# Holding transfers back during attention bursts, loading the third token tile ahead of the first query weights, and narrower last pieces, with a new table of shifts, in a fused attention and SwiGLU layer

## The chip, the cores and the metric

The kernel runs on one core of a Trainium2 chip. The metric is the device time in microseconds (us) of one execution. Times below are medians of several executions; a profile is one execution, and its span is about 1.7 us shorter than that execution's time. The engines are called PE (matrix products), DVE, ACT, POOL and SP, which here only issues transfers.

## The reference, cut to what matters

```python
# S = 2048 tokens, D = 1024, H = 32 heads of 32, N = 4 segments of L = 512, F = 3584, all bf16
for s in range(4):                       # per segment: local softmax and a memory of the past
    p = softmax(qs @ ks.T * scale + causal_mask);  a_dot = p @ vs
    a_mem = (phi(qs) @ M) / (phi(qs) @ z + 1e-6)
    o = g * a_mem + (1 - g) * a_dot
    M = M + phi(ks).T @ vs;  z = z + sum(phi(ks))
h  = x + o @ wo                          # q, k, v come from layernorm(x)
out = h + (silu(ln(h) @ w1) * (ln(h) @ w3)) @ w2
```

## The kernel before

The kernel writes operations into a graph. A small planner with its own cost model then decides the order on every engine, and a table SHIFT, with entries for 470 of 472 units of work, nudges that order. The table is the result of a search. What the chip does is fixed by the orders and the semaphores that the planner emits.

Attention of one segment and half of the heads (eight times in all) runs in ten *score tenancies* (products q k into four PSUM banks, then one exponential on ACT), with dense products of other stages between them, and then one *burst*: the denominators, four numerator columns j = 0 to 3, and in the first three segments the memory product of 64 small products.

```python
    def scores(self, s, g0, i, parts, at):           # one tenancy, i = 0..9
        ...
        o = self.mark = self.g.op("pe", 30.0 + 512 / 2.4, emit, reads=reads, cls=0, group=gr, gate="att")
        ...                                          # exponential on ACT, causal select on POOL

    def finish(self, s, half, at):                   # the burst
        ...
        column(Both(gd, gm) if gm else gd, range(4), lambda i, kc, j: self.ones32[:, j, :], ...)
        for j in range(4):
            gn.append(self.queue(j))
            column(gn[j], [j], lambda i, kc, j: v[:, kc, g0 + i, j, 0:32], j, ...)
        if gm:
            self.memory(s, half, gm)                 # 64 products of 33 columns, one operation
        ...

    def first_half(self):                            # the head
        ...
        loads = [(self.xs[t][:, :], self.x2d[t * 128:(t + 1) * 128, :]) for t in range(4)]
        loads.insert(2, (wq[:, :, 0:256], sq[:, :, 0:256]))
        loads.insert(5, (wk[:, :, 0:256], sk[:, :, 0:256]))
        ...
    # ffn_down, the tail:
        cols = [(0, 512), (512, 256), (768, 256)] if t == 15 else [(0, 512), (512, 512)]
```

The softmax here doesn't subtract the row's maximum and nothing guards it: scores larger than these inputs give would overflow.

Of the kernel before, what the change touches and what calls it, by code (L numbers as in the profile page):

```python
# [21 lines left out]
    0: (113, 0), 1: (-194, 1), 2: (-667, 0), 3: (-97, 0), 4: (-693, -1), 5: (-458, -1),  # L22
    6: (-38, 1), 7: (-273, 0), 8: (-32, 0), 9: (1616, 0), 10: (25, 1), 11: (-286, 1),
    12: (172, -1), 13: (-388, 0), 14: (-1163, 0), 15: (1, -1), 16: (-18, 0), 17: (-393, 0),
    18: (-432, 0), 19: (-332, -1), 20: (-726, 0), 21: (-980, 0), 22: (-590, 0), 23: (-337, 0),
    24: (386, 0), 25: (-423, 1), 26: (-992, 0), 27: (170, 1), 28: (-314, 0), 29: (108, -1),
    30: (-213, 0), 31: (-82, 0), 32: (72, 0), 33: (-46, 0), 34: (-61, 0), 35: (-15, 0),
    36: (66, 1), 37: (-122, 0), 38: (73, 0), 39: (75, 0), 40: (240, 1), 41: (790, 0),
    42: (436, -1), 43: (346, 1), 44: (-203, 0), 45: (-52, 1), 46: (280, 0), 47: (-138, 0),
    48: (-1000, 1), 49: (319, 0), 50: (244, 0), 51: (-194, 0), 52: (-341, 0), 53: (114, 1),  # L30
    54: (236, 0), 55: (443, 0), 56: (472, 0), 57: (-181, 0), 58: (202, 0), 59: (0, 1),
    60: (329, 0), 61: (176, 0), 62: (577, 0), 63: (232, 0), 64: (343, -1), 65: (62, -1),
    66: (-1, 0), 67: (-27, 0), 68: (380, -1), 69: (151, -1), 70: (672, 0), 71: (455, 0),
    72: (333, 0), 73: (389, -1), 74: (-231, 0), 75: (-215, 0), 76: (-1180, 1), 77: (-591, 0),
    78: (60, 0), 79: (105, 1), 80: (-645, 0), 81: (822, 0), 82: (720, 0), 83: (-36, 0),
    84: (290, 1), 85: (278, 0), 86: (781, -1), 87: (738, -1), 88: (264, 0), 89: (-38, 0),
    90: (255, 0), 91: (-292, 0), 92: (489, -1), 93: (276, 0), 94: (340, 0), 95: (-320, 0),
    96: (1003, 1), 97: (-984, 1), 98: (300, -1), 99: (545, 0), 100: (105, 1), 101: (-414, -1),
    102: (1239, 1), 103: (310, -1), 104: (-250, 0), 105: (18, -1), 106: (149, -1),
    107: (-967, 0), 108: (-407, -1), 109: (132, 0), 110: (198, 0), 111: (-185, 0),  # L40
    112: (-466, 0), 113: (484, -1), 114: (-58, 1), 115: (-243, -1), 116: (2, 0), 117: (-382, 1),
    118: (246, 0), 119: (-90, -1), 120: (796, 0), 121: (-239, 1), 122: (350, -1), 123: (22, -1),
    124: (-65, 0), 125: (-125, 0), 126: (75, -1), 127: (-802, 0), 128: (-162, -1),
    129: (-459, 0), 130: (609, 1), 131: (439, 0), 132: (287, 0), 133: (725, 0), 134: (-729, 1),
    135: (-763, 1), 136: (-378, 1), 137: (213, 0), 138: (552, 0), 139: (-94, 0), 140: (666, 0),
    141: (-279, -1), 142: (-1607, 0), 143: (103, 0), 144: (1000, 0), 145: (-281, 1),
    146: (-460, 0), 147: (-775, 0), 148: (-161, 0), 149: (-645, 0), 150: (-119, -1),
    151: (-271, -1), 152: (-125, 1), 153: (-757, 0), 154: (-45, 0), 155: (-1064, 1),
    156: (499, -1), 157: (272, -1), 158: (-539, -1), 159: (-398, 0), 160: (-178, 0),
    161: (-32, 0), 162: (-858, -1), 163: (136, 0), 164: (102, 0), 165: (541, 0), 166: (287, 0),  # L50
    167: (526, 1), 168: (-156, 0), 169: (143, 0), 170: (-57, 1), 171: (232, 0), 172: (-293, 0),
    173: (-111, 0), 174: (-244, 0), 175: (-566, 1), 176: (231, -1), 177: (-352, 0),
    178: (-672, 0), 179: (476, 0), 180: (318, -1), 181: (-30, 0), 182: (-1529, -1),
    183: (442, 0), 184: (314, -1), 185: (-580, 0), 186: (683, -1), 187: (261, -1),
    188: (-351, -1), 189: (-262, 0), 190: (-907, 0), 191: (122, 1), 192: (-381, 0),
    193: (-110, 1), 194: (704, 1), 195: (-226, -1), 196: (996, -1), 197: (-511, 1),
    198: (198, -1), 199: (-599, 1), 200: (-399, 1), 201: (519, 0), 202: (-310, -1),
    203: (10, -1), 204: (-305, 0), 205: (-354, 0), 206: (-422, 1), 207: (-148, 0),
    208: (-508, 0), 209: (-551, 0), 210: (377, 1), 211: (-139, 0), 212: (699, 0), 213: (378, 0),
    214: (236, 1), 215: (424, -1), 216: (-195, -1), 217: (-501, -1), 218: (-302, 1),  # L60
    219: (309, 0), 220: (-919, 0), 221: (321, -1), 222: (24, 1), 223: (-98, 0), 224: (619, 1),
    225: (593, 1), 226: (-320, -1), 227: (-779, -1), 228: (351, 0), 229: (327, 0),
    230: (524, 0), 231: (-389, -1), 232: (-574, 1), 233: (-315, 1), 234: (-277, -1),
    235: (469, 0), 236: (-369, 0), 237: (-511, -1), 238: (180, 0), 239: (-88, 0),
    240: (-241, -1), 241: (-5, 0), 242: (602, 1), 243: (304, 0), 244: (-787, 0), 245: (254, -1),
    246: (449, 0), 247: (1135, -1), 248: (-467, 1), 249: (-501, -1), 250: (130, 1),
    251: (-372, 1), 252: (-158, 0), 253: (1119, 0), 254: (-407, 0), 255: (30, 1), 256: (331, 1),
    257: (-413, 1), 258: (-309, 0), 259: (-293, 0), 260: (93, 1), 261: (200, 1), 262: (852, 0),
    263: (156, 0), 264: (168, 1), 265: (-419, 0), 266: (-101, -1), 267: (995, -1),
    268: (-504, 0), 269: (114, -1), 270: (-156, -1), 271: (230, 0), 272: (-118, 1),  # L70
    273: (-324, 0), 274: (313, 0), 275: (484, -1), 276: (408, -1), 277: (416, 0), 278: (127, 0),
    279: (41, 0), 280: (-85, 0), 281: (-440, 1), 282: (192, -1), 283: (-416, 0), 284: (490, -1),
    285: (-173, 0), 286: (73, -1), 287: (113, 0), 288: (162, 0), 289: (-231, 1), 290: (-91, -1),
    291: (-253, -1), 292: (-197, 0), 293: (-507, -1), 294: (98, 0), 295: (136, 0),
    296: (-846, -1), 297: (-281, -1), 298: (756, -1), 299: (605, 0), 300: (-49, -1),
    301: (266, 0), 302: (222, 0), 303: (163, 0), 304: (15, -1), 305: (7, -1), 306: (171, 1),
    307: (-102, 1), 308: (-164, 0), 309: (573, 0), 310: (36, 1), 311: (-391, -1), 312: (122, 0),
    313: (-258, 0), 314: (-377, -1), 315: (234, 0), 316: (-44, -1), 317: (1293, 1),
    318: (458, 0), 319: (-156, -1), 320: (284, 0), 321: (687, -1), 322: (-244, -1),
    323: (296, 0), 324: (-287, 0), 325: (503, -1), 326: (-600, 0), 327: (447, 0), 328: (409, 0),  # L80
    329: (-186, -1), 330: (17, -1), 331: (-46, 0), 332: (-745, -1), 333: (1259, 0),
    334: (1124, 0), 335: (-208, 0), 336: (-187, 0), 337: (-49, 1), 338: (-90, 0),
    339: (-801, 0), 340: (-433, 0), 341: (19, -1), 342: (229, 0), 343: (-749, 0), 344: (109, 0),
    345: (-144, 0), 346: (795, 0), 347: (79, 0), 348: (-554, 0), 349: (83, 0), 350: (-48, 0),
    351: (-26, -1), 352: (-38, -1), 353: (-200, 0), 354: (-529, 0), 355: (596, 1),
    356: (-272, 1), 357: (259, 0), 358: (330, -1), 359: (258, -1), 360: (345, -1),
    361: (444, 0), 362: (129, 0), 363: (915, 0), 364: (36, 1), 365: (280, 1), 366: (-192, 0),
    367: (208, 1), 368: (829, -1), 369: (19, -1), 370: (-310, -1), 371: (-643, 1),
    372: (-300, -1), 373: (109, 0), 374: (-186, -1), 375: (166, 1), 376: (-1088, 0),
    377: (-657, -1), 378: (-150, 0), 379: (36, 1), 380: (-532, -1), 381: (-323, -1),  # L90
    382: (554, 0), 383: (-401, 1), 384: (-833, 0), 385: (-135, -1), 386: (53, 0), 387: (16, 0),
    388: (548, 0), 389: (-612, 0), 390: (-525, 1), 391: (-475, 0), 392: (-658, 0),
    393: (339, 0), 394: (-515, -1), 395: (-70, -1), 396: (-258, -1), 397: (-860, -1),
    398: (47, 1), 399: (-616, 0), 400: (24, 0), 401: (56, 1), 402: (-245, -1), 403: (4, 1),
    404: (-199, 1), 405: (61, 1), 406: (-1407, -1), 407: (987, 0), 408: (544, 0), 409: (-76, 1),
    410: (194, 0), 411: (-100, -1), 412: (525, 0), 413: (-559, 0), 414: (1023, -1),
    415: (699, 1), 416: (498, 0), 417: (-583, 0), 418: (-521, 0), 419: (-287, 0), 420: (858, 0),
    421: (-596, 0), 422: (-482, 1), 423: (-82, 0), 424: (-41, 0), 425: (-14, 0), 426: (8, 0),
# [11 lines left out]
class Op:  # L110
# [6 lines left out]
    def __init__(self, engs, cost, emit, cls, seq):  # L117
# [16 lines left out]
        self.port = False  # L134
        self.patience = 0.0
        self.offered = 0.0
        self.unit = 0


class Group:  # L140
# [23 lines left out]
class Graph:  # L164
# [128 lines left out]
    def dma(self, out, in_, cls=5, deps=(), eng="sp"):  # L293
        n = 1
# [1084 lines left out]
```

## Time and profile before

| | before |
|---|---|
| time, median of the first 3 runs | 896.3 us |
| span in the profile | 895.0 us |
| PE busy | 880.6 us |
| 512-column products begin (head) | 18.07 us |
| last product ends, span ends (tail) | 892.42, 895.0 us |

The prediction below reads this profile line by line. In a list of groups a line has the engine, the line of the program, output<-inputs, and times; a wait line has who waited <- for what: total us, times, longest us; a chain line has start, duration, and what the end of the program hung on then. In a busy table each engine has its busy time in the stretch, and PE's granted clock, the DMA share and GB/s follow at the end. The timeline of the kernel before has the last addition:

```profile
892.44 0.42 DVE L1289 TENSOR_TENSOR ob<-hr,ps 128x256 bf16<-128x256 bf16 x1 [0.89 <-PE ps L708]
```

### The profile page before, as it was taken

Reading aid. Unit: us, or ns where it says so; the run is one execution under the profiler, and the core shown is the slowest. Engines: PE = TensorE matmul, PEld = TensorE weight load, DVE = VectorE, ACT = ScalarE, POOL = GpSimd, SP = SyncE. Lnnn points to the kernel's source line nnn. Section 1 sums busy time; section 2 is a strip of 40 time slices with the busy share of each in tenths; the row PEclk is TensorE's granted clock in tenths of the full one; section 3 lists DMA queues with packets and bytes.
Section 4 is the critical chain, followed back from the end, with each engine's and each line's share of the span. In section 5 each row is a group of like instructions: output and inputs, shape, how many; then the busy total and the mean of one; then the engine's idle time right before and its main releaser. Section 6 shows DMA issues by size and latency. Waiting matters only on the chain.

```text
span 895.0 us, 13604 instructions
## 1 busy us (share of the span) xinstructions
PE 880.6 (98%) x5833; PEld 403.4 (45%) x5921; DVE 417.6 (47%) x631; ACT 287.9 (32%) x306; POOL 173.8 (19%) x226
## 2 busy tenths in 40 slices
PE   8999999999999999999999999999999999999998
PEld 5343444444444444444444444444444444444445
DVE  5784848585848485754555311211334333331111
ACT  6767766656565646111111100000111111110000
POOL 2553445353534343100200000000000000000000
PEclk9999999999999999999999999999999999999999
DMA  7899755634541221753475211113223221301110
GB/s 235 227 212 271 187 142 147 187 92 130 165 99 57 72 70 58 225 153 92 120 224 140 85 36 36 30 46 90 64 60 94 71 71 48 95 24 41 40 37 30
DMA packets 146540, 96.32 MB, mean 108 GB/s; under 512 B 45488, under 2 KB 133680, under 8 KB 146480
## 3 DMA queue, kind: packets, MB, share of 16 engines
q1 hardware_dynamic: 146480, 95.45, 38.8%
q8 instruction: 47, 0.77, 0.4%
q14 instruction: 13, 0.11, 0.0%
HBM read 76.55 MB, written 8.39 MB: 95 GB/s over the span
## 4 chain that ended last, share of the span: by engine, by line
PE 97%; issue 1%; DVE 1%; DMA 1%; ACT 0%; SPq 0%; ACTq 0%; DVEq 0%
PE ps L708 89%; PE ps L1107 4%; PE ps L1057 3%; DMA xs<-in_A_x_dram 1%; PE ps L985 0%; PE ps L1184 0%; ACT et L1069 0%; PE ps L1100 0%; DVE t L1260 0%; DVE hm L1265 0%; PE ps L720 0%; SPq L299 0%; DVE R L1163 0%; ACT sg L1257 0%; DVE Nsb L1171 0%
## 5 line engine op out<-in xcount | busy, mean ns | idle before, releaser
L708 PE MATMUL ps<-hnT,w1b 128*128 128x512 bf16 x876 | 218.4, 379 | 1.4 <-issue 0.3
L708 PE MATMUL ps<-hnT,w3b 128*128 128x512 bf16 x873 | 217.4, 379 | 1.5 <-issue 0.5
L1257 ACT ACTIVATE sg<-ps 128x512 bf16<-128x512 f32 x112 | 66.9, 597 | 403.1 <-PE ps L708 403.1
L708 PE MATMUL ps<-w2b,hm 128*128 128x512 bf16 (+1 forms) x907 | 195.3, 372 | 0.9
L1069 ACT ACTIVATE et<-ps 128x2048 bf16<-128x2048 f32 x80 | 150.0, 1875 | 39.3 <-PE ps L1057 38.9
L1260 DVE SCALAR_TENSOR_TENSOR t<-sg,ps 128x512 bf16<-128x512 bf16 x112 | 76.8, 685 | 169.4 <-ACT sg L1257 169.2
L708 PEld LDWEIGHTS ps<-w2b,hm 128*128 128x128 bf16 x924 | 90.4, 98 | 103.2
L708 PEld LDWEIGHTS ps<-hnT,w1b 128*128 128x128 bf16 x896 | 86.5, 98 | 105.5 <-issue 8.2
L708 PEld LDWEIGHTS ps<-hnT,w3b 128*128 128x128 bf16 x896 | 86.5, 98 | 105.4 <-issue 2.9
L1078 POOL TENSOR_SCALAR_AFFINE_SELECT et<-et 128x512 bf16<-128x512 bf16 x96 | 84.0, 881 | 126.2 <-ACT et L1069 126.0
L1265 DVE SCALAR_TENSOR_TENSOR hm<-t,ps 128x512 bf16<-128x512 bf16 x112 | 76.7, 686 | 50.5 <-PE ps L708 47.9
L1289 DVE TENSOR_TENSOR ob<-hr,ps 128x512 bf16<-128x512 bf16 (+1 forms) x33 | 22.1, 671 | 143.0 <-PE ps L708 143.0
L708 PE MATMUL ps<-wo,oT 128*128 128x512 bf16 x249 | 60.7, 380 | 0.6 <-issue 0.3
L708 PE MATMUL ps<-xnT,wp 128*128 128x512 bf16 (+1 forms) x345 | 59.7, 320 | 1.4 <-issue 0.6
L708 PE MATMUL ps<-hnT,wp 128*128 128x512 bf16 x250 | 59.0, 380 | 0.7 <-issue 0.6
L708 PEld LDWEIGHTS ps<-xnT,wp 128*128 128x128 bf16 x352 | 27.7, 98 | 26.9 <-issue 3.6
L708 PEld LDWEIGHTS ps<-wo,oT 128*128 128x128 bf16 x256 | 23.9, 98 | 29.8 <-issue 2.9
L708 PEld LDWEIGHTS ps<-hnT,wp 128*128 128x128 bf16 x256 | 23.6, 98 | 29.8 <-issue 3.8
L1200 POOL TENSOR_TENSOR oT<-Nsb,R 128x512 bf16<-128x512 f32 x23 | 35.8, 1569 | 4.1 <-DVE R L1197 4.1
L1163 DVE STREAM_TRANSPOSE R<-Rc 128x1024 f32<-128x1024 f32 x28 | 33.6, 1222 | 0.1
L1229 DVE TENSOR_TENSOR h<-h,ps 128x512 bf16<-128x512 bf16 x32 | 21.7, 680 | 25.1 <-PE ps L708 24.9
L1057 PE MATMUL ps<-qT,kT 32*128 32x128 bf16 (+3 forms) x512 | 31.7, 301 | 0.0
(82 smaller groups left out, 520.9 us busy)
## 6 DMA issues: line engine op xcount, KB each, us to landing
w1b<-in_B_w_dram SPq DMA_DIRECT2D x28, 512.0 KB, 3.9
w3b<-in_B_w_dram SPq DMA_DIRECT2D x28, 512.0 KB, 3.8
wp<-in_A_wv_dram SPq DMA_DIRECT2D x8, 1024.0 KB, 5.5
wp<-in_A_wq_dram SPq DMA_DIRECT2D x7, 1024.0 KB, 5.9
wp<-in_A_wk_dram SPq DMA_DIRECT2D x7, 1024.0 KB, 5.7
w2b<-in_B_w_dram SPq DMA_DIRECT2D x7, 1024.0 KB, 8.0
xs<-in_A_x_dram SPq DMA_DIRECT2D x16, 256.0 KB, 5.6
h<-in_A_x_dram SPq DMA_DIRECT2D x16, 256.0 KB, 3.7
```

Of the source, the lines that this page charges most:

```text
L708: return [e.matmul(p[0](gr), p[1], p[2], start=p[3], stop=p[4]) for p in part]
L1057: ins.append(e.matmul(self.bank(gr, j, 512 - 128 * kc, off), k[r, g0 + g, 128 * kc:128 * kc + 128], q[r, g0 + g, 128 * kc:512], start=True ...
L1069: return [e.activation(et[:, :, :], src, AF.Exp, scale=self.scale)]
L1078: self.pool_op(lambda e, v=v, pat=pat: e.affine_select(v, v, pattern=pat, compare_op=ALU.is_ge, fill=0.0, base=0, channel_multiplier=-1), ...
L1107: ins.append(e.matmul(self.ps[32 * i:32 * i + 32, b * 512 + 128 * kc:(b + 1) * 512], lhsT(i, kc, j), at[i, kc][:, j, :], start=kc == 0 and ...
L1163: return self.dve_op(lambda e: e.transpose(out, src), dve_ns(1024), [Rc[:, t, 2 * n:2 * n + 2, :]], [dst], 2)
L1200: self.either(lambda e, out=out, Ns=Ns, R1=R1: e.tensor_tensor(out, Ns, R1, op=ALU.add), 512, 2, [Ns, R1], [out], 2)
L1229: self.g.op("dve", dve_ns(512), lambda e, gr, hs=hs: [e.tensor_tensor(hs, hs, self.bank(gr), op=ALU.add)], reads=[hs], writes=[hs], cls=1, ...
L1257: self.g.op("act", act_ns(512), lambda e, gr, sg=sg: [e.activation(sg, self.bank(gr), AF.Tanh, scale=0.5)], writes=[sg], cls=0, group=gg)
L1260: e.scalar_tensor_tensor(t1, sg, 1.0, self.bank(gr), op0=ALU.add, op1=ALU.mult)], reads=[sg], writes=[t1], cls=0,
L1265: e.scalar_tensor_tensor(dst, t1, 0.5, self.bank(gr), op0=ALU.mult, op1=ALU.mult)], reads=[t1], writes=[dst], cls=0,
L1289: self.g.op("dve", dve_ns(n), lambda e, gr, hs=hs, ob=ob, n=n: [e.tensor_tensor(ob, hs, self.bank(gr, 0, n), op=ALU.add)], reads=[hs], wri ...
```

## The change

Its intent has three parts. (1) In the plan, no transfer is issued from score tenancy 9 to the numerator product of j = 3, and transfers offered meanwhile get a dependence on that product. (2) Tile 2 of x is loaded before the first query weights, and the planner is given measured scales for the first loads. (3) The last 256 columns of the last tile become two pieces of 128. A new table SHIFT was searched for the changed planner.

```diff
 SHIFT = {
-    0: (113, 0), 1: (-194, 1), 2: (-667, 0), 3: (-97, 0), ...      (nearly every entry differs; cut)
+    0: (60, 1), 1: (-213, 0), 2: (8, 0), 3: (-400, 0), ...
 }
@@ schedule()
                 for e in ENGINES:
-                    if not free[e]:
+                    if not free[e] or e == "sp" and hush:
                         continue
...
                     started.add(o)
+                    hush = o.hush or hush
...
+            if not events and hush:
+                hush = None
+                continue
...
                 n_done += 1
+                if x is hush:
+                    hush = None
+                    for _, _, o in avail["sp"]:
+                        o.deps.setdefault(x, True)
@@ first_half()
+        x = [(self.xs[t][:, :], self.x2d[t * 128:(t + 1) * 128, :]) for t in range(4)]
+        loads = [x[0] + (1.04,), x[1] + (0.7,), x[2] + (1.2,),
+                 (wq[:, :, 0:256], sq[:, :, 0:256], 1.54), x[3] + (0.65,), ...]
@@ scores()
+        if i == 9:
+            self.final = o
@@ finish()
+        self.final.hush = self.mark
@@ ffn_down()
-            cols = [(0, 512), (512, 256), (768, 256)] if t == 15 else [(0, 512), (512, 512)]
+            cols = [(0, 512), (512, 256), (768, 128), (896, 128)] if t == 15 else [(0, 512), (512, 512)]
```

## The prediction

> **What bounds the kernel now.** I read the page first, then the busy time by stretch, the engine waits of PE, the chain of waits, and the timelines of the head, of one burst and of the tail.
>
> From the page:
>
> ```profile
> span 895.0 us, 13604 instructions
> PE 880.6 (98%) x5833; PEld 403.4 (45%) x5921; DVE 417.6 (47%) x631; ACT 287.9 (32%) x306; POOL 173.8 (19%) x226
> PE   8999999999999999999999999999999999999998
> PEclk9999999999999999999999999999999999999999
> DMA  7899755634541221753475211113223221301110
> ```
>
> PE is busy 98% at full clock; only the first and last slices are below 9. At most 895.0 - 880.6 = 14.4 us is idle. A change of transfers and order, with the same products, can win no more unless products themselves get shorter.
>
> The busy time by stretch says where the 14.4 us lie (the first two columns are the stretch and its length, the third is PE's busy time):
>
> ```profile
> 0.00:22.40 22.40, 18.40 (x195) 12.29 (x197) 12.04 (x34) 13.63 (x26) 5.06 (x22) 1.00 0.77 235
> 200.00:300.00 100.00, 97.61 (x921) 42.95 (x930) 66.55 (x94) 63.13 (x56) 46.02 (x52) 1.00 0.41 112
> 500.00:600.00 100.00, 99.53 (x456) 45.39 (x464) 17.33 (x26) 4.18 (x7) 0.00 (x0) 1.00 0.15 43
> 800.00:895.00 95.00, 91.93 (x447) 44.42 (x454) 12.93 (x20) 0.60 (x1) 0.00 (x0) 1.00 0.12 37
> ```
>
> Idle: 4.0 us in the head, 3.07 in the last stretch, and 0.47 per 100 us in the pure feed-forward part (500 to 600). The 0.47 isn't a wait: the chain shows runs of 49 products of 10.74 us, each 10.79 after the one before, so one record in 50 is missing. In 200 to 300 it is 2.39, the largest of the middle. The engine waits of PE name what is left:
>
> ```profile
> PE ps L708 <- issue: 3.0, 19, 0.2
> PE ps L720 <- DVE xs L862: 2.1, 2, 1.2
> PE ps L708 <- DVE oT L773: 1.2, 1, 1.2
> PE ps L985 <- issue: 1.1, 1, 1.1
> PE ps L708 <- DMA wp<-in_A_wq_dram: 0.4, 1, 0.4
> ```
>
> The 19 waits of 0.16 us follow a change between tiled and full-array products and stay. What the change can touch is one gap of 1.1 us at L985 (the memory product), the head's 2.1 + 0.4, and the tail.
>
> The gap, in the chain of waits between 262 and 276 us:
>
> ```profile
> 266.68 2.72 PE ps L1107 x80
> 269.39 0.34 PE ps L985 x42
> 269.73 1.07 issue
> 270.81 0.32 PE ps L985 x22
> ```
>
> The 64 memory products are one operation without a semaphore inside, yet PE stops after 42. Nothing of the program can hold it there: what is missing is the next instruction. In 264 to 271 us the DMA view has one fetch of instructions, an x load that takes 4.6 us to land (median of its kind on the page 3.7) and a transposing transfer that takes 7.4 (median 3.9). The transfers were issued inside the burst.
>
> **The Trainium skill.** (1) "Runtime: NRT & Kernel Launch", Instruction fetch mechanics: instructions stream in 16 KiB blocks of 256, fetched over a DMA queue of the engine's own; crossing a block is "mostly hidden". The trace has such fetches, and here one probably wasn't hidden: the slice 50 to 60 us with its burst takes 216 products and 217 weight loads, an ordinary 10 us 61. (2) "DMA: Bandwidth & Descriptors", Queues, rings and completion order: each DMA engine takes turns between queues, a packet at a time; so a fetch shares with data. The late landings agree with sharing, and don't prove it. (3) "TensorEngine Tiling (Array Packing)", Key Properties: a change of tiling mode drains the engine. Agrees: four dense products take 0.86 us, and a score tenancy starts 0.96 us after four of them began (60.77 to 61.73), so some 0.1 us a change. (4) "DMA: Bandwidth & Descriptors", Specifications: under 512 B a transfer does read-modify-write. The last pieces' rows fall from 512 to 256 B; nothing of this size is in the trace to compare.
>
> **The change, part by part.**
>
> *Silence in the burst.* In the planned order no transfer is issued from score tenancy 9 of a burst to its last numerator product; those offered meanwhile get a dependence on that product, so the silence is real on the chip. No instruction goes. It removes whatever slows fetches in eight bursts. In this trace just one stalled: 1.07 us at most. The others ran 64 memory products in about 0.52 us without a gap, though transfers were in flight at 49.4 to 50.7 (two weights, one x) and 171 to 176 (two weights). I count 0.8 of the 1.07, since the fetch itself remains: **-0.85 us**.
>
> *Head.* Loads go x0, x1, x2, wq, x3, wk instead of x0, x1, wq, x2, x3, wk. The timeline of DVE shows why:
>
> ```profile
> 6.87 0.42 DVE L732 COPY xnT<-ps 128x512 bf16<-128x512 bf16 x1 [0.24 <-PE ps L720]
> 8.34 1.29 DVE L831 BATCH_NORM_STATS2 lnst<-xs 128x6 f32<-128x512 bf16 x2 [1.05 <-DMA xs<-in_A_x_dram]
> 9.55 0.72 DVE L862 TENSOR_SCALAR xs<-xs,lnst,rstd 128x512 bf16<-128x512 bf16 x2
> ```
>
> Tile 1's scale is ready at 7.19 + 0.57 = 7.76 (POOL), but in DVE's order tile 2's statistics stand before its application, and tile 2 lands only at 8.32; so it is applied at 9.55 and PE transposes it at 10.00, after 1.23 us idle. wq lands at 7.70, x2 0.62 later. With the order turned, x2 lands before 6 (x0 at 3.49, x1 at 4.14, so some 0.65 apart, to at most about 1.2) and wq near 7.70 + 0.65 = 8.35. DVE no longer waits: tile 2's statistics fit from 6.6, tile 1 is applied near 8.4, its transposes run near 8.8. PE pays the later wq: idle from 7.30 to about 8.35 instead of 7.70, +0.65; it wins the 1.23 and the 0.20 before 10.92. Net -0.8 at most. But tile 3 still lands at about 9.06 and its chain through ACT sets its transposes at 14.45. After them PE did 52 products in 2.90 us; 32 of them (1.8 us) need tile 3, so only 20 x 0.056 = 1.1 us can come forward. The cap doesn't bind, but a new short wait between tiles is likely. I take **-0.55 us**.
>
> *Tail.* Tile 15's last 256 columns become two pieces of 128. Last addition: 0.69 us at 512, 0.42 at 256; in a straight line 0.29 at 128, -0.13. Transfer: 1.7 us for 128 KB, 1.6 for 64 KB; 32 KB would be 1.55, but may lose it to 256 B rows: 0. PE: 28 products of 256 columns (about 109 ns: half of 213 plus 2.6) become 56 of 128 at 55.8 (1.34 us for 24 in the head), +0.07; there are as many more weight loads, which in the head kept up. Net **-0.05 us**.
>
> *Shifts of all units.* Nearly every entry differs. With PE full between 20 and 887 us, an order can only alter the number of mode changes (80 score tenancies and eight bursts stay) and create waits. I give it **+0.1**; the held transfers below cost +0.2.
>
> Sum: -0.85 - 0.55 - 0.05 + 0.3 = -1.15. A change of this sort is usually kept because it helped, and short issue gaps may go with it; I choose -1.5: 896.3 - 1.5 = **894.8 us**.
>
> **The rivals.** (a) *The silence moves the wait.* Up to three transfers per burst start 5 to 9 us later, together. From 22 to 100 us the DMA share is 1.00 at 240 GB/s, so there a pause isn't free. A weight tile of 1 MB takes 5.5 to 5.9 us to land; with three buffers and 32 products of 216 ns (6.9 us, stretched by attention) on each there are some two tiles of slack, over 13 us. So it should be hidden; if not, one late tile costs 2 to 5 us: 896 to 900. (b) *Transfers were innocent*: the gap is a chance of where a block of instructions ends, so it stays or moves to another burst; then the gain is only head and tail, 895.5 to 896. (c) *The head doesn't gain*: the later wq eats it, +0.65 against 1.43; 895.2 to 895.7. (d) *PE products get faster without transfers*, as if they contended for memory: 49 (with the missing one, 50) in 10.79 us is 216 ns at a DMA share of 0.15 and 1.0 alike (four in 0.86 at 60 us), which speaks against it.
>
> **Range and chances.** Best case: 1.07 + 1.1 + 0.2 + 0.6 of small gaps = 3.0, hence 893.3. Worst likely: one new wait, 896.8. Range **893.3 to 896.8**. Two per cent is 17.9 us, more than all idle time: faster 0.005. Slower by as much would need several starved weights: 0.01. Within: 0.985.
>
> **What would show it.** Right: PE busy within 1 us of 880.6; no issue gap over 0.3 us in the eight bursts; no DMA issue on SP between the tenth score tenancy and the last numerator; PE's transposes of tile 1 before 9.2 us, the wait for wq near 1 us, and the 512-column work starting near 17.4 instead of 18.07; last addition about 0.29. Wrong: PE waits for wp, hnT or wo over 0.5 us after a burst (rival a), a 1 us issue gap anywhere (b), or a head that ends at 18 (c). A busy PE changed by over 3 us would break the ledger itself.

## The result

The changed kernel took 895.03 us (median of 4 runs, 894.24 to 895.94) against 896.49 us (4 runs, 896.26 to 898.08): 1.46 us less. A ratio is the mean time of one kernel's runs over that of the other's of the same rounds, so it isn't quite the ratio of the medians: 0.998, with an interval of 0.9963 to 0.9998. The profiled run of the changed kernel was its fastest (894.24 us), so its span of 892.5 us flatters it by almost 1 us.

The page of the changed kernel, then its busy table (stretch, length, PE, weight loads, DVE, ACT, POOL, clock, DMA share, GB/s):

```profile
span 892.5 us, 13660 instructions
PE 881.4 (99%) x5862; PEld 404.4 (45%) x5949; DVE 426.3 (48%) x645; ACT 282.2 (32%) x296; POOL 171.6 (19%) x223
```

```profile
0.00:22.40 22.40, 20.55 (x206) 13.25 (x208) 13.44 (x34) 14.12 (x26) 5.73 (x23) 1.00 0.79 237
200.00:300.00 100.00, 98.78 (x932) 43.33 (x941) 66.67 (x98) 62.61 (x53) 47.46 (x55) 1.00 0.39 108
```

PE's busy time is as before within 0.8 us: the change took away idle time, not products. In 200 to 300 us PE gained 98.78 - 97.61 = 1.17 us. Its engine waits, with the line L989 of the memory product gone from the list:

```profile
PE ps L711 <- issue: 3.3, 21, 0.2
PE ps L711 <- DVE oT L776: 1.2, 1, 1.2
PE ps L711 <- ACT xnT L734: 0.4, 1, 0.4
```

The timeline shows the memory product of burst 6 in one piece of 0.69 us (64 products; before, 42, then a gap, then 22), and in the head and the tail DVE's lines that answer to those shown before:

```profile
262.95 0.69 PE L989 MATMUL ps<-v,pkn 128*32 128x33 bf16 x64
...
6.36 1.28 DVE L834 BATCH_NORM_STATS2 lnst<-xs 128x6 f32<-128x512 bf16 x2
8.45 0.73 DVE L865 TENSOR_SCALAR xs<-xs,lnst,rstd 128x512 bf16<-128x512 bf16 x2 [0.57 <-POOL rstd L861]
...
890.22 0.29 DVE L1296 TENSOR_TENSOR ob<-hr,ps 128x128 bf16<-128x128 bf16 x1 [0.83 <-PE ps L711]
```

The 2.5 us between the two spans, cut at two marks that both traces have (the start of the 512-column products and the end of the last product):

| stretch | before | after | difference |
|---|---|---|---|
| start to the first 512-column product | 18.07 | 16.99 | -1.08 |
| from there to the end of the last product | 874.35 | 873.21 | -1.14 |
| from there to the end | 2.58 | 2.30 | -0.28 |

So the total was as predicted, and the differences lie in the stretches that it named. Whether for its reasons is what the experiments ask.

### The profile page after: what moved, and what is told of

Same layout as the page of the kernel before. It is cut to its first block, busy times and chain, and to the rows that moved or that the text cites. A ratio compares the mean times of both kernels' runs of the same rounds, so it can differ in the third digit from the quotient of the medians.

```text
span 892.5 us, 13660 instructions
## 1 busy us (share of the span) xinstructions
PE 881.4 (99%) x5862; PEld 404.4 (45%) x5949; DVE 426.3 (48%) x645; ACT 282.2 (32%) x296; POOL 171.6 (19%) x223
## 4 chain that ended last, share of the span: by engine, by line
PE 97%; issue 1%; DVE 1%; ACT 0%; DMA 0%; POOL 0%; SPq 0%; DVEq 0%; ACTq 0%
PE ps L711 90%; PE ps L1113 4%; PE ps L1061 3%; DMA xs<-in_A_x_dram 0%; PE ps L989 0%; PE ps L1191 0%; PE ps L723 0%; PE ps L1106 0%; DVE t L1267 0%; ACT oT L823 0%; ACT sg L1264 0%; ACT oT L820 0%; DVE T L1139 0%; DVE hm L1272 0%; DVE Nsb L1159 0%
## 5 line engine op out<-in xcount | busy, mean ns | idle before, releaser
L711 PE MATMUL ps<-w2b,hm 128*128 128x512 bf16 (+2 forms) x935 | 195.4, 366 | 0.9
L1296 DVE TENSOR_TENSOR ob<-hr,ps 128x512 bf16<-128x512 bf16 (+2 forms) x34 | 22.3, 655 | 142.8 <-PE ps L711 142.8
L1207 POOL TENSOR_TENSOR oT<-Nsb,R 128x512 bf16<-128x512 f32 x21 | 31.4, 1515 | 11.4 <-PE ps L711 6.3
L711 PE MATMUL ps<-wp,xnT 128*128 128x512 bf16 x124 | 31.1, 380 | 0.4 <-issue 0.2
```

Source lines behind the costliest of these rows:

```text
L711: return [e.matmul(p[0](gr), p[1], p[2], start=p[3], stop=p[4]) for p in part]
L1207: self.either(lambda e, out=out, Ns=Ns, R1=R1: e.tensor_tensor(out, Ns, R1, op=ALU.add), 512, 2, [Ns, R1], [out], 2)
L1296: self.g.op("dve", dve_ns(n), lambda e, gr, hs=hs, ob=ob, n=n: [e.tensor_tensor(ob, hs, self.bank(gr, 0, n), op=ALU.add)], reads=[hs], wri ...
```

## The experiments

**How fetches of instructions were read.** The trace also has the transfers of the instruction queue of PE, one per 256 instructions. To set them against the program I numbered PE's instructions in the program's order (a product is two, a weight load and a matmul; a separate wait is one) and matched them to the weight loads in the trace, none of which is missing. The gap of the kernel before then stands right before instruction 5313, and 5313 = 20 x 256 + 193. In the kernel before each of the 47 fetches falls within 4.5 us of the moment when PE passes a number 193 + 256 k, one fetch for each such number; taken in this order, each brings the block that begins at the next one. This gives, per burst, when PE entered a block, when the fetch of the next one ran, and when PE went on with that next block. The rows here are worked out in this way from the traces of all runs of this section:

```
run              burst  enters block  fetch ran         went on   fetch later by   gap
before             6     266.13      268.55 - 269.52    270.80        2.42        1.07
after              6     260.73      260.57 - 261.53    263.47       -0.16        none
before_hold        6     277.65      277.81 - 278.84    281.07        0.16        none
before_hold1       6     266.10      268.34 - 269.49    270.80        2.25        1.10
before_holdT       6     266.76      268.22 - 269.30    270.60        1.47        0.2
before_shift72     1      56.09       59.04 -  60.25     61.46        2.95        1.91
before_shift72     2      96.49      100.16 - 101.25    102.83        3.67        3.09
after_noise        4     170.93      174.45 - 175.41    176.80        3.52        2.15
after_noise        6     263.86      266.43 - 267.49    269.00        2.56        2.21
after_nohush       5     214.14      220.63 - 221.63    223.03        6.49        1.20
```

Wherever there is a gap, it stands at a number of the form 193 + 256 k, and PE goes on 1.2 to 1.6 us after the record of the fetch ends. A late fetch alone makes no gap: in the changed kernel three fetches at bursts 1, 2 and 4 come 3.8, 3.5 and 4.0 us late, but their blocks last 9.2, 7.8 and 15.3 us, and PE doesn't stop. The block of burst 6 lasts 2.75 us there, and its fetch is prompt.

**1. Move the ends of the blocks (before_shift72).** Nothing but the place of the block ends changes.

```diff
             ins = o.emit(engine, o.group)
+            if e == "pe" and o.pos == 0:
+                for _ in range(144):              # emitted as 72 instructions
+                    engine.wait_ge(sems["dve"], 1)
```

> The kernel before with 72 more instructions on PE that only look at a semaphore already reached, right after the 12 warm-up products, in time that PE spends waiting for x; every order and transfer is as before, only the ends of the 256-instruction blocks move by 72. Theory (a block of instructions that runs out in a burst faster than the next one is fetched): the gap at product 43 of the memory product of burst 6 is gone; block ends now stand 24 products after the memory product of burst 2 and 35 after that of burst 1, so a gap of 0.5 to 2 us comes at one or both of those places, and the time is within 1 us of before, either way. Rival (something in burst 6 itself, as a hazard or the DVE): the gap stays in burst 6 after 42 memory products.

Measured: 905.69 us (ratio 1.0097). The chain of waits in bursts 1 and 2:

```profile
57.92 1.10 PE ps L1110 x32
59.02 0.54 PE ps L711 x2
59.56 1.91 issue
...
98.81 0.93 PE ps L1110 x23
99.73 3.09 issue
```

The gap in burst 6 is gone, and two larger ones stand where they were foretold: 34 products after the memory product of burst 1 and 23 after that of burst 2 (35 and 24 were named). PE lacks instructions there; nothing in burst 6 itself is at fault. The expected time was wrong by 8 us: the two gaps cost 5.0 us, the 72 instructions held the head up by 2.7 us (a third gap of issue; the clock fell there too, to 0.50 in 10 to 12 us), and after the 3.09 us gap the clock was halved. The busy table (PE alone, then clock, DMA share, GB/s) shows it:

```profile
102.00:104.00 2.00, 1.17 (x11) 0.50 0.65 148
104.00:106.00 2.00, 2.00 (x6) 0.50 0.82 216
```

**2. Put transfers into the bursts of the changed kernel (after_noise).** Two useless copies of 1 MB, issued after score tenancy 9 of bursts 4 and 6.

```diff
+    for b in (3, 5):
+        first = self.bursts[b]                     # score tenancy 9
+        for k in range(2):
+            ...                                    # dma scratch <- x, 512 rows, deps = {first: True}
```

> The changed kernel with two useless 1 MB copies from x to a scratch in memory, issued when the last score tenancy of burst 4 and of burst 6 is done (the result stays right, no order changes). Theory: they delay the fetch in those bursts. In burst 6 the fetch now starts 0.2 us before PE enters the block and ends 1.9 us before PE needs the next; it comes 1 to 3 us later, and a gap of 0.5 to 2.5 us shows where the block ends, just after the memory product of burst 6, perhaps another in burst 4; span 0.5 to 3 us longer than the changed kernel. Rival (transfers innocent): no gap over 0.3 us in these bursts, span within 0.3 us unless PE waits for a named transfer.

Measured: 899.23 us (ratio 1.0025). The chain of waits in burst 4, then 6:

```profile
174.35 0.30 PE ps L1009 x37
174.65 2.15 issue
...
266.26 0.52 PE ps L1009 x64
266.78 2.21 issue
```

Both fetches come 3.5 and 2.6 us late, and PE has two gaps of 4.4 us together. Against the span of 893.8 us in experiment 5, which ran on the same chip with the same orders on the other engines, its 898.0 us are 4.2 us longer, more than the 0.5 to 3 expected because both bursts stalled. Transfers in a burst, here plain copies, delay the fetch, and this makes the gap: shown.

**3. The silence alone (before_hold).** All orders of the kernel before stay; only the waits are added.

```diff
+    for first, last in self.bursts:                # tenancy 9, numerator j = 3
+        for o in sp:
+            if first.start <= o.start < last.start and all(u.start >= last.start for u in o.users):
+                o.start = last.start + 1e-6 * k    # keeps SP's order
+                o.deps[last] = True
```

> The kernel before with every engine's order untouched; only the transfers that its plan starts between score tenancy 9 of a burst and that burst's numerator product j=3 get a wait on that product (the change's silence and nothing else). Theory (the 1.07 us gap in the memory product of burst 6 is PE short of instructions, because the fetch of the next block queued behind transfers issued in the burst): the fetch that started 2.4 us after PE entered block 5057 starts within 0.5 us of it, the gap at L985 is gone, span 0.7 to 1.2 us shorter than the kernel before. Rival (transfers innocent, the gap belongs to the place where the block ends): the gap stays at about 1.1 us and the time is the same within 0.3 us. Second rival (the silence moves the wait): gap gone, but PE waits over 0.5 us for a weight or hnT.

Measured: 914.67 us, ratio 1.02 (1.0187 to 1.0214). The fetch is prompt and the gap gone (third row of the table), but the engine waits of PE now begin so:

```profile
PE ps L723 <- DMA hnT<-hn: 4.7, 1, 4.7
PE ps L723 <- DMA wp<-in_A_wv_dram: 4.7, 1, 4.7
PE ps L723 <- DMA h<-in_A_x_dram: 3.2, 2, 2.8
PE ps L735 <- DVE xs L877: 1.5, 2, 1.0
PE ps L723 <- DMA wp<-in_A_wq_dram: 1.5, 1, 1.5
```

For late transfers PE waits 4.7 + 4.7 + 3.2 + 1.5 = 14.1 us, all but 0.3 of it right after a burst, and after the two long waits the clock falls (0.62 and 0.53 in the two stretches of 4 us after 188 us), which lengthens the products there. First theory and second rival are both true: the silence heals the gap, and by itself moves more wait than it heals.

**4. Which transfer? (before_hold1, before_holdT).** In burst 6 of the kernel before three transfers are in the way: w3b (issued 262.70), the transposing transfer hnT (263.12) and an x load (266.40). Of the held ones, one run holds the last alone, the other the transposing one alone.

```diff
-    for first, last in self.bursts: ...
+    first, last = self.bursts[5]
+    held = [o for o in sp if first.start <= o.start < last.start]
+    held[-1].start = last.start + 1e-6             # before_holdT: held[-2]
+    held[-1].deps[last] = True
```

> The kernel before, all orders untouched; of all transfers just one, the 256 KB x load of burst 6 (issued at 266.4 us, landing 4.6 us later), waits for that burst's numerator product j=3. Theory that this load delayed the fetch: the fetch of the next block starts under 1 us after PE enters block 5057 instead of 2.4, the gap of 1.07 us at L985 is below 0.3 us, and no weight is late, so 0.7 to 1.2 us shorter than the kernel before. Rival (the transposing transfer issued at 263.1 us delayed it): the fetch still comes over 2 us late and the gap stays near 1 us; time the same.

Measured: 896.57 us, ratio 0.9995 (0.9983 to 1.0007), the same. I named the x load as the cause, and it isn't: in the chain of waits the gap stays.

```profile
269.36 0.34 PE ps L997 x42
269.70 1.10 issue
```

> The kernel before with one transfer of burst 6 held until numerator product j=3: the transposing transfer of normalised rows (hnT) that was issued at 263.1 us and took 7.4 us to land; the x load of that burst goes ahead of it. All other orders are untouched. Theory (the transposing transfer delayed the fetch): the fetch starts under 0.7 us after PE enters block 5057 instead of 2.4, the 1.1 us gap at L985 is gone; but PE needs this hnT right after the burst and waits 4 to 5 us for it, with the clock down for some us after that, so 3 to 8 us slower. Rival (the w3b load of 262.7 us did it): the fetch still comes over 2 us late and the gap stays.

Measured: 900.5 us, ratio 1.0029. From the engine waits of this run:

```profile
PE ps L720 <- DMA hnT<-hn: 3.5, 1, 3.5
...
PE ps L997 <- issue: 0.2, 1, 0.2
```

With hnT out of the way the gap falls from 1.07 to 0.2 us, so the transposing transfer made most of this gap, in one profile each. Of the lateness it made less: the fetch is still 1.5 us late, against 2.4, and not under 0.7 as expected. The w3b and x loads that stay have a share (the x load now goes out at 263.80 us instead of 266.40), which with all three held (experiment 3) is gone too. PE needs this hnT right away and waits 3.5 us for it.

That plain transfers suffice is seen in experiment 2, and in burst 2 of before_shift72, where PE entered the block at 96.49 us. SP's timeline has

```profile
94.94 0.39 SPq L299 DMA_DIRECT2D wp<-in_A_wv_dram  x1
98.94 4.04 SPq L306 DMA_TRANSPOSE pkn<-pk  x2
```

so the fetch (100.16) was already 2.4 us late when the first transposing transfer of that stretch was issued.

**5. The added waits without effect on orders (after_nowait).** The line that gives held transfers their dependence is left out; the planned orders stay, which was compared instruction by instruction.

```diff
                     hush = None
-                    for _, _, o in avail["sp"]:
-                        o.deps.setdefault(x, True)
```

> The changed kernel with all orders untouched and only the added waits of the silence left out (they bind in bursts 1, 2, 3 and 4 only; in 5 to 8 this order has no transfer to hold). Theory: fetches in bursts 1 to 4 start later (by 0.5 to 2 us), but those blocks have 2.5 us and more of slack, so no stall or one below 0.5 us; time within 0.4 us of the changed kernel, so 1.1 to 1.6 us below the kernel before. Rival (the waits themselves are the gain): about 1 us slower than the changed kernel, with an issue gap of about 1 us in one of bursts 1 to 4.

Measured: 895.08 us, ratio 0.998 (0.9967 to 0.9993), the ratio of the changed kernel itself. The waits bind nowhere that matters. What the silence did, it can only have done in the planning, together with the new table; which of the two keeps burst 6 free isn't separated. In burst 6 of the changed kernel the last issue before the burst (258.92 us) is the one at 253.47.

**6. Plan without the silence (after_nohush).** `self.final.hush = self.mark` is left out, everything else including the table stays, and the planner runs anew.

> The changed kernel with the silence taken out of the planning as well, so that transfers may be issued in a burst and everything after it is planned anew with the same table of shifts. Theory (a gap comes where a transposing transfer is issued in a burst whose block of instructions runs out in under 4 us): the table was not made for it, so some wait of PE over 0.5 us appears and it is 0.5 to 6 us slower than the changed kernel; if a gap of issue appears in a burst, a hnT or pkn transfer was issued within 4 us before it. Rival (the silence is worth nothing): within 0.5 us of the changed kernel.

Measured: 901.11 us, ratio 1.0048, against 896.17 us for the changed kernel in the same rounds. PE waits longest for a weight (wk, 1.5 us), and a gap of issue is back, now in burst 5. The chain of waits, then SP's timeline:

```profile
221.83 1.20 issue
```

```profile
213.50 1.75 SPq L299 DMA_TRANSPOSE hnT<-hn  x1
...
217.83 0.38 SPq L292 DMA_DIRECT2D wp<-in_A_wk_dram  x1
220.53 2.02 SPq L299 DMA_TRANSPOSE hnT<-hn  x1
```

Two transposing transfers stand in this stretch, the second 1.3 us before the gap, with plain ones between them (h, h_scr, and a weight of 1 MB), and the fetch is 6.5 us late. Which of them delayed it can't be told from this run. The rest of the 4.9 us are other waits, of a table that wasn't made for this plan; so the 4.9 us aren't the worth of the silence.

**7. The new parts with the old table (after_oldshift).** Only SHIFT is the old one.

> The changed kernel (silence, new order of the loads, narrow pieces) with the table of shifts of the kernel before. Theory (the silence by itself only moves the wait, the new table is what keeps PE fed): PE waits for held transfers for over 3 us in total, and it is slower than the kernel before by 3 us or more. Rival (the table is noise): within 1 us of the changed kernel.

Measured: 942.96 us, ratio 1.0514. The first engine wait of PE is

```profile
PE ps L719 <- DMA h<-in_A_x_dram: 14.5, 2, 10.3
```

followed by 8.5 us for exponentials of ACT in nine waits. The longest of these, in PE's timeline:

```profile
525.94 9.07 PE L719 MATMUL ps<-wo,oT 128*128 128x512 bf16 x31 [10.27 <-DMA h<-in_A_x_dram]
```

Attention was over by then (its last numerator product is at 378 us), and so was every silence. The theory, over 3 us of waits for held transfers, isn't shown: the waits that may be such are those for query, key and value weights, 3.1, 1.4 and 0.6 us. The old table spoils the whole plan. It isn't a detail: with it the changed kernel is 46 us slower than the kernel before; but this doesn't say what the new table is worth by itself. The reverse, the old kernel with the new table, and the old kernel with the new loads and their scales, could not be built: the planner runs into a deadlock with them. So the parts can't be told apart by switching them one by one.

**8. The order of the first loads (before_swap, after_swap).** Only the places of tile 2 and wq in SP's order are exchanged, after the planning.

```diff
+        sp = self.order["sp"]
+        a, b = sp[2], sp[3]
+        a.start, b.start, a.pos, b.pos = b.start, a.start, b.pos, a.pos
+        sp[2], sp[3] = b, a
```

> The kernel before with one exchange in SP's order: tile 2 of x is issued before the first query weights. All other orders are untouched. Theory of the head: DVE does not wait for tile 2 any more, tile 1 is applied near 8.5 us instead of 9.55, PE transposes it near 8.9 instead of 10.0, and the 512-column work starts 0.7 to 1.1 us earlier than 18.07; time 0.5 to 1.1 us below the kernel before. Rival (the later weights eat the gain): PE waits for wq over 0.7 us longer, and the time is the same within 0.3 us.

Measured: 896.43 us against 897.15, ratio 0.9994 (0.9982 to 1.0005), not to be told from the same. Tile 1 is applied at 8.55 us, as expected, but the engine waits of PE then show

```profile
PE ps L712 <- DMA wp<-in_A_wk_dram: 1.0, 1, 1.0
PE ps L712 <- DMA wp<-in_A_wq_dram: 0.9, 2, 0.7
```

The 512-column products begin at 17.51 us. Five profiles of the kernel before or its variants with the same head have 18.07, 17.82, 17.58, 18.18 and 17.11 (before_hold), mean 17.75: 0.24 us, well within their scatter.

> The changed kernel with the exchange undone in SP's order alone: first query weights before tile 2. Theory: DVE and PE wait for tile 2 again, the 512-column work starts 0.7 to 1.1 us later than the 16.99 of the changed kernel, time 0.5 to 1.1 us above it. Rival: within 0.3 us of the changed kernel.

Measured: 896.02 us, ratio 0.9984 (0.9971 to 0.9998). Its six runs fall into two groups, told by the mean clock: 894.42, 895.02 and 895.24 us at 1.0, and 896.79, 897.15 and 897.46 us at 0.998. The profile caught the second. Busy table, with the clock third from the end:

```profile
8.00:10.00 2.00, 0.61 (x11) 0.44 (x8) 1.84 (x5) 1.26 (x3) 0.00 (x0) 1.00 1.14 321
10.00:12.00 2.00, 1.97 (x20) 1.87 (x21) 1.78 (x6) 1.49 (x5) 0.85 (x3) 0.57 1.11 289
```

PE waits 1.4 us for tile 1 and works only 0.61 of 2 us; then its clock is nearly halved for 4 us. The two groups differ by 897.13 - 894.89 = 2.2 us; the trace's record of the clock has half speed for 3.41 us, which can make 1.7 of them at most. Without such a fall the exchange changes nothing that the times show: 894.89 us is the mean of its undisturbed runs, and the changed kernel's median was 895.03, though in other rounds, where the kernel before was 0.7 us faster. Whether the exchange makes the fall more frequent (3 runs of 6, against 1 of 9 of the changed kernel) is too few runs to tell.

**9. The narrow pieces (before_tail).** Only `cols` of the last tile is changed.

> The kernel before with only the last 256 columns of the last tile as two pieces of 128. Theory: the last addition takes 0.29 instead of 0.42 us, PE's last 56 products cost some 0.07 us more than the 28 did, so the time is 0.0 to 0.15 us below the kernel before and not to be told from it. Rival (256-byte rows make the last store slow): 0.2 us or more above, with a last store that takes over 1.6 us to land.

Measured: 897.04 us, ratio 0.9998 (0.9986 to 1.001): the same, as expected. In its trace the last addition takes 0.29 us, the last store 1.5 us to land (1.6 before), and from the start of the last addition to the end pass 896.0 - 893.74 = 2.26 us instead of 2.56. That is 0.3 us at the very end, less 0.07 for the narrower products by the prediction's sum. No time shows it.

**10. The changed kernel again (after_again).**

> The changed kernel once more, on the same chip and in the same rounds as the runs beside it: 1.0 to 2.2 us below the kernel before.

Measured: 896.17 us against 897.09, ratio 0.9986 (0.9973 to 0.9998). In the profiled run wq kept PE waiting 1.1 us in the head, the clock fell there as in after_swap, and the 512-column products began at 18.92 us instead of 16.99. From that mark to the end it took 894.4 - 18.92 = 875.5 us, and 892.5 - 16.99 = 875.5 us in the first profile. So these two runs differ by what happens before that mark, and by nothing else.

No version tried beats the changed kernel; after_nowait and after_swap equal it within the noise.

## Why the prediction was right

The total (-1.5 us) came out at -1.46 in the medians and at about -0.2% and -0.14% in the two sets of rounds, and the direction is clear of noise, just: the interval runs from 0.02% to 0.37%, or 0.2 to 3.3 us. That the number was met so closely is luck in part: the steps add up to -1.15 us, and the rest of the -1.5 was a guess that a change of this sort is usually kept because it helped. In the second set of rounds the medians differ by 0.92 us. By its steps:

- **What bounds.** Right: PE busy changed from 880.6 to 881.4 us, and what was gained was idle time.
- **Silence in the burst, -0.85.** The mechanism was right in kind: a late fetch of instructions, delayed by transfers (experiments 1 and 2), and the whole gap went, 1.07 us in the first pair of profiles. It was somewhat undersized: the profiles of kernels with the old order in burst 6 have 1.1, 1.1, 1.5 and 1.4 us. That is about the whole measured gain. Two things in the step were wrong. The silence "is real on the chip" only in part: the product j = 3 isn't the last numerator product to run, so in bursts 1 to 4 of the changed kernel transfers are issued in the middle of the burst (in burst 3, two value weights from 125.70 us, with PE in the burst from 124.93 to 130.22), and nothing comes of it: the blocks there leave the fetch time, or the fetch has begun before (burst 4: fetch 170.11, first issue 170.65). And the waits aren't what helps (experiment 5), the order is. The sign it named, no issue between tenancy and last numerator, is therefore false.
- **Head, -0.55.** The wait of DVE for tile 2 was read rightly and vanished. The -1.08 us of the first pair of profiles can't be put down to the order of the loads: the exchange by itself moves the mark by less than its scatter, and the times don't show it. With the whole new head the mark is at 16.99, 16.54 (after_nowait), 16.87 (after_noise) and 18.92 us (after_again), mean 17.33 against 17.75: -0.4, near the -0.55, with a scatter that is larger. The price it named, a wait for wq near 1 us, is missing in the first profile, where PE has no wait for wq, and was paid in before_swap (0.9, and 1.0 for wk) and after_again (1.1). What it lacked is the clock: in after_swap the runs that lost it took 2.2 us more, and in after_again the mark came 1.9 us later than in the first profile.
- **Tail, -0.05.** About -0.2 by the traces; the last stretch shortened by 0.28 us and not by 0.13, as the smaller store also landed sooner. Too small for the times.
- **Shifts of all units, +0.1, and held transfers, +0.2.** The mid part after removal of the gap was -1.14 + 1.07 = -0.07 us, so neither cost showed up. But calling the shifts nearly worthless misread them: a table fits the plan that it was searched for, and with the old one the changed kernel loses 46 us, in waits all over the plan. Waits without new orders cost +18 us (experiment 3).
- **Rival (a)**, that the silence moves the wait, is true of the silence and false of the change. The estimate of two tiles of slack was wrong where it was tried: a held weight came 4.7 us late, and so did hnT. **Rival (b)** is half true: where a block ends decides whether a late fetch is felt, and the transfers decide whether it is late; it takes both. **Rival (c)**, that the head doesn't gain, isn't excluded: experiment 8 can't tell the exchange from nothing. **Rival (d)** found no support in these runs.

Open: whether a transposing transfer holds up a fetch more than a plain one of its size (no run compares them), and whether they meet with the fetch on one DMA engine. In the times, head and tail can't be told from nothing.

## What to carry to other kernels

When an engine stops in the middle of one operation without a semaphore, count its instructions: gaps that stand one fetch block apart, or a multiple of it, point to a missing fetch, and a run with shifted block ends tests it. Keep transfers, plain ones too, out of the few microseconds before a stretch of very short instructions, but do it by planning them earlier: the waits that only held them here moved more time than they saved. On a bound PE look also at what follows a gap: after the one of 3.09 us the clock was at half for 6.83 us by the trace's record, up to 3.4 us more.

## What the Trainium skill lacked or had wrong

- "Runtime: NRT & Kernel Launch", Instruction fetch mechanics, holds fetches to be mostly hidden and gives PE room for 2048 instructions as well as two blocks in all. The runs fit two blocks: where a block was short, a fetch that came 1.5 to 6.5 us late stopped PE at the very next block end, for 0.2 to 3.1 us, and every gap of this kind was at 193 + 256 k. It doesn't say how long a fetch takes: 0.9 to 2.1 us in the records of all runs here (1.0 to 1.2 in the table), and 1.2 to 1.6 us more until PE went on.
- "DMA: Bandwidth & Descriptors" has the turns between queues, but no size for what a fetch loses by them: one transposing transfer, most of 1.07 us of gap in burst 6; two plain 1 MB copies, 2.2 us.
- "TensorE: Matmul & The Clock Gate", HAM oscillation, gives the rule that gaps over some 3.4 us let the clock fall. Here it fell after one gap of 3.09 us, and in the head after waits of 1.4 us (after_swap, with PE busy 0.61 of 2 us) and 1.1 us (after_again) beside smaller ones; in after_swap in 3 runs of 6, which took 2.2 us more than the others.
- No page that I read says outright that a separate wait on PE counts in the fetch block; 72 of them moved the gaps, and held the head up by 2.7 us.
